# A hand-ordered attention and two-expert kernel on one core: a new order for all of its tasks, written out as a table

## Chip, core and metric

The kernel runs on one core of a Trainium2 chip. Five engines work at once: TensorE (PE in the profile, with PEld for its weight loads), VectorE (DVE), ScalarE (ACT), GpSimd (POOL) and SyncE (SP), which issues all the DMA transfers of this kernel. Each engine takes its own instructions strictly in the order in which the program lists them, and waits on semaphores for the others. The metric is the device time of one execution in microseconds (us); lower is better.

## What is computed

```python
# B, H, S, D = 2, 8, 768, 64: attention masked by equal hash buckets of 6 bits
q_bits = (np.einsum('bhsd,dk->bhsk', q, proj) > 0)          # k_bits alike
mask = q_bucket[:, :, :, None] == k_bucket[:, :, None, :]
scores = np.where(mask, scale * (q @ k.T), -1e9)
attn = exp(scores - max); attn = attn / (sum(attn) + 1e-09); out = attn @ v
# first expert layer, x: 1536 tokens x 512, FF 1536
xn = x / rms * rms_g;  y = (silu(xn @ w_gate) * (xn @ w_val)) @ w_out
# second expert layer, FF 2048
h = y @ w_in;  result = where(h > 0, h, exp(min(h, 0)) - 1) @ w_out2
```

All inputs but the expert matrices are fp32; the expert matrices arrive as 64-bit floats. To keep precision, a matrix product is done in three passes over a high part ("hi", rounded to the matmul's fp32r) and a rest ("lo" = value minus hi): hi*hi, lo*hi, hi*lo.

## The kernel before

**Attention.** The 16 heads are worked as 8 pairs. For a pair, `load_x` loads q and k, transposed to 128 rows (`qk`, `kk`, `qq`: 64 rows of each of two copies). `prep` makes the operands: bits of the hash (`ps_b`, `bitt`), one-hot rows of the mask (`ps_c`, "hot" rows), and the hi and lo parts of k (`operand_k`, tile `tk`) and q (`operand_q`, tile `tq`). A tile `tq` has hi in rows 64 to 127, lo in rows 0 to 63, a second copy of hi ("dup", brought by a small DMA) and the hot rows, so that scores, mask and both precisions come out of four matmuls per 128 queries (`ps_s`, `score`). Then VectorE takes the row maximum (L477, tile `nm`), ScalarE the exponential with its row sum (L487, `p`, `sums`), TensorE transposes p (`ps_p`, `turn`), ScalarE and VectorE (L523, L527; for some tiles ScalarE and GpSimd, L532 to L539) split it into hi and lo (`pt`), TensorE multiplies by v (`ps_v`, `weigh`), and L576 and L580 join the parts. There are 12 score tiles per pair, 96 in all. `post` adds 1e-9 to the 12 row sums of the pair (L598), inverts them (L603), spreads them (`rw`, `ps_x`), and scales the result into `xT` (L629); squares are summed for the norm (`sq`, `ps_z`). `norm` runs after pair 4 for the first batch, on GpSimd, and after pair 8 for the second, on VectorE.

**Experts.** Matrices come in groups of two or three blocks of 128 hidden units (`weights`). Each half matrix is one DMA into `wraw` (L790); ScalarE (L804) and four VectorE instructions (L807, L813, L820, L827) turn the 64-bit words into fp32 (`wf`), ScalarE casts hi (L849, `whi`), GpSimd subtracts for lo (L853, `wlo`). This set of four VectorE instructions is called a conversion below. Then follow `ps_h` (L902), the activation, `ps_y` (L987), and for the second layer `ps_h` and `ps_o` (L1042).

**What sets the order.** Every piece of work is a task (`plan.add`: engine, estimated microseconds, function, keys read and written, priority). `Plan.order` simulates the engines at build time and picks, each time, the task that can start first, with ties broken by priority; the table `OFF` shifts the priorities. `GATE0` names the pair whose first score must be issued before the first group's matrices may load. Buffers are pools of fixed size: 22 `slot` tiles (operands, `p`, `wraw`, `whi`, `wlo`), 14 `h3` tiles.

Of the kernel before, what the change touches and what calls it, by code (L numbers as in the profile page):

```python
# [20 lines left out]
GATE0 = 4  # L21
# [12 lines left out]
class Plan:
# [40 lines left out]
    def order(self):  # L75
        n = len(self.tasks)
        users = [[] for _ in range(n)]
        left = [0] * n
        for i, t in enumerate(self.tasks):
            left[i] = len(t[3])  # L80
            for d in t[3]:
                users[d].append(i)
        free = {tag: [0.0] * c for tag, c in self.caps.items()}
        pending = {b: len(ts) for b, ts in self.touch.items()}
        last = {b: 0.0 for b in self.touch}
        held = set()
        clock = {}
        table = None
        busy = {}
        ready = {}  # L90
        at = [0.0] * n
        end = [0.0] * n

        def put(i):
            eng = self.tasks[i][0]
            clock.setdefault(eng, 0.0)
            ready.setdefault(eng, []).append(i)

        for i in range(n):
            if not left[i]:  # L100
                put(i)
        out = []
        while len(out) < n:
            best = None
            for eng, lst in ready.items():
                now = clock[eng]
                fits = []
                for i in lst:
                    _, us, fn, deps, bufs, prio, lat, tab = self.tasks[i]
                    t = max(now, at[i])  # L110
                    need = {}
                    for b in bufs:
                        if b not in held:
                            need[b[0]] = need.get(b[0], 0) + 1
                    ok = True
                    for tag, c in need.items():
                        fr = free[tag]
                        if len(fr) < c:
                            ok = False
                            break  # L120
                        t = max(t, max(fr[:c]))
                    if ok:
                        fits.append(((t, prio), i))
                if fits:
                    (t, prio), i = min(fits)
                    key = (t, prio, i, eng)
                    if best is None or key < best:
                        best = key
            assert best is not None, "no task can start"
            t, _, i, eng = best  # L130
            _, us, fn, deps, bufs, prio, lat, tab = self.tasks[i]
            ready[eng].remove(i)
            for b in bufs:
                if b not in held:
                    held.add(b)
                    free[b[0]].pop(0)
            if eng == "PE":
                k = int(t / self.WINDOW)
                full = us
                if k < self.COLD or (k > self.COLD and busy.get(k - 1, 0.0) < self.ACTIVE * self.WINDOW):  # L140
                    us = min(2 * us, max(us, us + 0.5 * ((k + 1) * self.WINDOW - t)))
                rate = self.duty[i] * full / us if us else 0.0
                a = t
                while a < t + us:
                    k = int(a / self.WINDOW)
# [1081 lines left out]
```

## Time and profile before

| | |
|---|---|
| runs | 853.52, 851.31, 851.55 us; median 851.55 |
| the profiled execution | 854.81 us by its own time; its span, first to last instruction, 853.0 us |
| busy share of the span | PE 96%, PEld 84%, DVE 73%, ACT 50%, POOL 38% |
| mean granted TensorE clock | 0.988 of full speed |

A busy share is a mean over two very different stages: attention (roughly the first 306 us, to the last `ps_z`) and the experts (the rest). A PE that is busy is not a PE at its peak, since matmuls overlap in the pipeline and a slower clock also counts as busy.

### The profile page before, as it was taken

To read this page: it belongs to the slowest core of one execution; us is meant where nothing else is said; L and a number is where in the kernel's file an instruction comes from. 1 tells how busy PE (TensorE), PEld (TensorE's weight loads), DVE (VectorE), ACT (ScalarE), POOL (GpSimd) and SP (SyncE) were. 2 spreads that over 40 slices of the span, in tenths; PEclk is the share of its full clock that TensorE was granted. 3 is DMA by queue.
4 is the path that set the end of the run, shared out by engine and by line. 5 is a ranking of instruction groups with operands and counts; after the bars stand their busy time and mean duration, and the time that the engine had idled before them with its cause. 6 is when DMAs were issued, how large, how long until landed. Compare 5 with 4: busy or idle time off the path is not lost.

```text
span 853.0 us, 11879 instructions
## 1 busy us (share of the span) xinstructions
PE 822.4 (96%) x4498; PEld 718.0 (84%) x4498; DVE 621.2 (73%) x941; ACT 428.3 (50%) x787; POOL 321.0 (38%) x247
## 2 busy tenths in 40 slices
PE   6989999999889889999999999999999999999998
PEld 5878899888779879989889898888888888888886
DVE  4788899999999997343283665678957778676754
ACT  3868898988688654332231322335544332332321
POOL 6979936578989921121011221210201111111100
PEclk8989999999999989999999999999999999999999
DMA  6334424543102201110210321113222121101003
GB/s 209 102 137 148 149 85 130 168 139 106 54 1 75 75 1 38 62 39 37 74 50 1 114 85 62 42 70 111 75 75 57 58 72 50 50 25 59 16 10 138
DMA packets 28474, 64.99 MB, mean 76 GB/s; under 512 B 2817, under 2 KB 3585, under 8 KB 28417
## 3 DMA queue, kind: packets, MB, share of 16 engines
q1 hardware_dynamic: 28416, 64.24, 23.2%
q8 instruction: 35, 0.57, 0.3%
q14 instruction: 23, 0.18, 0.1%
HBM read 57.94 MB, written 3.15 MB: 72 GB/s over the span
## 4 chain that ended last, share of the span: by engine, by line
PE 65%; DVE 8%; POOL 1%; issue 1%; ACT 1%; DVEq 0%; ACTq 0%
PE ps_h L902 37%; PE ps_o L1042 15%; PE ps_y L987 12%; DVE nm L477 2%; DVE pt L527 1%; DVE wf L820 1%; DVE wf L807 1%; DVE wf L827 1%; PE ps_v L562 1%; ACT pt L523 0%; DVE xT L629 0%; DVE ot L580 0%; PE ps_p L515 0%; POOL xT L724 0%; PE ps_z L667 0%
## 5 line engine op out<-in xcount | busy, mean ns | idle before, releaser
L853 POOL TENSOR_TENSOR wlo<-wf,whi 128x768 fp32r<-128x768 f32 (+1 forms) x54 | 92.3, 1718 | 432.0 <-ACT whi L849 366.7
L902 PE MATMUL ps_h<-xn,whi 128*128 128x512 f32 (+2 forms) x768 | 191.3, 338 | 1.5 <-DVE ot L580 1.5
L902 PEld LDWEIGHTS ps_h<-xn,whi 128*128 128x128 f32 x768 | 134.7, 190 | 14.2 <-DVE ot L580 2.0
L902 PE MATMUL ps_h<-xn,wlo 128*128 128x256 f32 (+2 forms) x384 | 129.3, 337 | 0.0
L1042 PE MATMUL ps_o<-whi,h 128*128 128x512 f32 (+1 forms) x388 | 118.5, 387 | 0.0
L902 PE MATMUL ps_h<-y,whi 128*128 128x512 f32 x384 | 118.2, 389 | 0.0
L927 ACT ACTIVATE sg<-ps_h 128x512 f32<-128x512 f32 (+1 forms) x87 | 50.7, 582 | 117.1 <-PE ps_h L902 115.1
L948 ACT CAST h<-hf 128x512 fp32r<-128x512 f32 (+1 forms) x87 | 51.6, 605 | 113.7 <-DVE hf L933 62.2
L562 PE MATMUL ps_v<-pt,vv 128*128 128x256 f32 x576 | 94.3, 296 | 7.9 <-DVE pt L527 5.2
L477 DVE TENSOR_REDUCE nm<-ps_s 128x1 f32<-128x768 f32 x96 | 90.8, 949 | 11.3 <-PE ps_s L470 10.9
L487 ACT ACTIVATE p<-ps_s,nm 128x768 f32<-128x768 f32 x96 | 87.4, 911 | 21.0 <-DVE nm L477 19.8
L470 PE MATMUL ps_s<-tk,tq 128*128 128x384 f32 x384 | 91.3, 362 | 5.3 <-POOL tq L374 2.2
L562 PEld LDWEIGHTS ps_v<-pt,vv 128*128 128x128 f32 x576 | 79.2, 190 | 15.4 <-DVE pt L527 8.7
L987 PE MATMUL ps_y<-h,whi 128*128 128x512 f32 (+1 forms) x312 | 90.9, 373 | 0.0
L952 DVE TENSOR_TENSOR h<-hf,h 128x512 fp32r<-128x512 f32 (+1 forms) x87 | 67.5, 790 | 27.1 <-ACT h L948 26.5
L515 PE MATMUL ps_p<-ident,p 128*128 128x128 f32 x576 | 82.1, 277 | 4.9 <-ACT p L487 1.5
L1042 PEld LDWEIGHTS ps_o<-whi,h 128*128 128x128 f32 x388 | 72.5, 188 | 15.1 <-DVE oa L1054 0.2
L902 PEld LDWEIGHTS ps_h<-y,whi 128*128 128x128 f32 x384 | 72.1, 188 | 15.1
L527 DVE TENSOR_TENSOR pt<-ps_p,pt 128x512 fp32r<-128x512 f32 x120 | 79.2, 682 | 7.3 <-ACT pt L523 6.4
L849 ACT CAST whi<-wf 128x768 fp32r<-128x768 f32 (+1 forms) x54 | 39.1, 733 | 84.3 <-DVE wf L827 71.9
L902 PEld LDWEIGHTS ps_h<-xn,wlo 128*128 128x128 f32 x384 | 73.1, 190 | 5.7
L515 PEld LDWEIGHTS ps_p<-ident,p 128*128 128x128 f32 x576 | 66.6, 142 | 12.4 <-ACT p L487 2.3
(91 smaller groups left out, 1401.8 us busy)
## 6 DMA issues: line engine op xcount, KB each, us to landing
wraw<-in_moe_w_out_dram SPq DMA_DIRECT2D x12, 768.0 KB, 4.6
qk<-in_heads_dram SPq DMA_DIRECT2D x16, 384.0 KB, 3.5
kk<-in_heads_dram SPq DMA_DIRECT2D x16, 384.0 KB, 5.3
qq<-in_heads_dram SPq DMA_DIRECT2D x16, 384.0 KB, 5.7
wraw<-in_moe_w_in_dram SPq DMA_DIRECT2D x8, 768.0 KB, 4.6
wraw<-in_moe_w_out_dram SPq DMA_DIRECT2D x10, 512.0 KB, 3.4
vn<-in_v_dram SPq DMA_DIRECT2D x8, 384.0 KB, 3.6
wraw<-in_moe_w_gate_dram SPq DMA_DIRECT2D x4, 768.0 KB, 4.5
```

Source lines behind the costliest of these rows:

```text
L470: nc.tensor.matmul(st[B_][:, hf, 0:HS], lhsT=tq[:, x, c * 128:(c + 1) * 128], rhs=tk[:, x, hf * HS:(hf + 1) * HS], start=(x == 0), stop=(x ...
L477: nc.vector.tensor_reduce(out=st["nm", u, cc], in_=st[B_][:, :, 0:HS], axis=AX.XY, op=ALU.max, negate=True,)
L487: nc.scalar.activation(out=halves(st["p", u][:, cc]), in_=st.pop(B_)[:, :, 0:HS], func=AF.Exp, bias=st["nm", u, cc], scale=1.0, accum_out= ...
L515: nc.tensor.transpose(out=st[B_][:, o:o + 128], in_=p[:, cc, (2 * n + kt) * 128:(2 * n + kt + 1) * 128], identity=ident,)
L527: nc.vector.tensor_tensor(out=pt[:, 1], in0=st.pop(B_), in1=f(pt[:, 0]), op=ALU.subtract)
L562: nc.tensor.matmul(st[B_][:, 0:256], lhsT=st["vv", j][:, a, 2 * n + kt, :], rhs=pt[:, x, kt * 256:(kt + 1) * 256], start=(n == seq[0] and ...
L853: nc.gpsimd.tensor_tensor(out=l, in0=s["w"], in1=f(h), op=ALU.subtract)
L902: nc.tensor.matmul(ps[:, o:o + ln], lhsT=w[wp][:, kk, ft * 128:(ft + 1) * 128], rhs=t[xp][:, s:s + ln], start=(kk == 0 and n == 0), stop=( ...
L948: nc.scalar.copy(out=st["h", g, blk, ft][:, 0, 0:bw], in_=s["hf"])
L952: nc.vector.tensor_tensor(out=h[:, 1, 0:bw], in0=s["hf"], in1=f(h[:, 0, 0:bw]), op=ALU.subtract)
L987: nc.tensor.matmul(s["ps"][:, 0:bw], lhsT=wo[wp][:, ft, m * 128:(m + 1) * 128], rhs=h[:, xp, 0:bw], start=(ft == 0 and i == 0), stop=(ft = ...
L1042: nc.tensor.matmul(s["ps"], lhsT=h[:, xp, t * 128:(t + 1) * 128], rhs=wo[wp][:, ft, ds], start=(ft == 0 and i == 0), stop=(ft == n - 1 and ...
```

## The change

- The order of all 2,732 tasks is written out as a list, `ORDER`; `Plan.order` is gone, and `run` follows the list. `OFF` has other numbers, and is no longer used to order.
- `GATE0` goes from 4 to 2 (counted from 0): the first group's loads may be issued from the third pair on, before from the fifth.
- The hi part of q, before one GpSimd instruction on 128 rows with a scale per row from the tile `share` (L354, scale 1 above, 1/8 below), becomes two GpSimd instructions on 64 rows: a copy (`upper`) and a multiplication by a constant (`lower`). The dup DMA now waits for `lower` alone, lo for `upper` alone.
- The addition of 1e-9 to the 12 sums goes from VectorE to GpSimd.
- Estimates in `plan.add` change; they no longer have an effect once the order is a list.

```diff
-GATE0 = 4
+GATE0 = 2
...
-QENG = [("Pool", "SP", "Pool", "Pool")] * 16
...
+QENG = ["Pool"] * 16
...
+ORDER = [
+    9, 0, 6, 5, 1, 7, 56, 50, 53, 2, 8, 48, 51, 57, 59, 49, 28, 10, 12, 13, 14, 15, 16, 17, 54, 55, 11, 60, 61, 68,
...
-    def order(self):
...
     def run(self):
-        for i in self.order():
+        assert sorted(ORDER) == list(range(len(self.tasks)))
+        for i in ORDER:
             self.tasks[i][2]()
...
-        def hi():
-            cast(engs[0], operand(j, a, 0)[:, 0, cs], st["x", j, a, 2][:, cs], share[:, 1:2])
...
+        def upper():
+            out, in_ = operand(j, a, 0)[up, 0, cs], st["x", j, a, 2][up, cs]
+            nc.gpsimd.tensor_copy(out=out, in_=in_)
+
+        def lower():
+            out, in_ = operand(j, a, 0)[dn, 0, cs], st["x", j, a, 2][dn, cs]
+            if how == "mixed":
+                nc.scalar.activation(out=out, in_=in_, func=AF.Copy, scale=QSCALE)
             else:
...
+                nc.gpsimd.tensor_scalar(out=out, in0=in_, scalar1=QSCALE, scalar2=None, op0=ALU.mult)
...
+        his, los, dups = ([okey(j, a, 0, (p, h)) for h in cols] for p in ("hi", "lo", "dup"))
...
+            plan.add("Pool", 0.12 + n * 0.00092, upper, [X_], los, prio)
...
+                plan.add("Pool", 0.12 + n * 0.00092, lower, [X_], his, prio)
+        dma(dup, 64 * n * 4, his, dups, prio)
+        plan.add("Pool", pool(n), lo, [X_], los, prio)
...
         def plus():
             st[R_] = sml.tile([128, 2, NC], F32, tag="r", name="r")
-            nc.vector.tensor_scalar(
+            nc.gpsimd.tensor_scalar(
                 out=st[R_], in0=st["sum", j], scalar1=1e-9, scalar2=None, op0=ALU.add,
             )
...
-        plan.add("DVE", 0.18, plus, sums, [R_], prio)
+        plan.add("Pool", 0.12, plus, sums, [R_], prio)
```

The line numbers of the changed kernel are 47 or 48 higher in most places (L477 becomes L524, L527 L574, L807 to L827 L854 to L874, L629 L676, L647 L694).

**GpSimd, first pair.** Its first instructions that work on q and k, before:

```order
L334 TENSOR_TENSOR tk<-kk,tk 64x384
L354 TENSOR_SCALAR tq<-qq,share 128x384 x2
L374 TENSOR_TENSOR tq<-qq,tq 64x384 x2
L334 TENSOR_TENSOR tk<-kk,tk 64x384
L293 CAST vv<-vn 128x6x64 x2
L299 TENSOR_TENSOR vv<-vn,vv 128x6x64 x2
```

and now (L405 is `upper`, L412 `lower`, L420 q's lo, L382 k's lo):

```order
L405 CAST tq<-qq 64x384 x2
L420 TENSOR_TENSOR tq<-qq,tq 64x384
L412 TENSOR_SCALAR tq<-qq 64x384 x2
L420 TENSOR_TENSOR tq<-qq,tq 64x384
L382 TENSOR_TENSOR tk<-kk,tk 64x384 x3
L405 CAST tq<-qq 64x384 x2
L412 TENSOR_SCALAR tq<-qq 64x384
L341 CAST vv<-vn 128x6x64 x2
```

The first head's q now comes before all of k; before, k's first half stood ahead of it. On SP the first transfer is now `qq` (before the sixth), and the two `qk`, before first and second, are second and fourth.

**VectorE, end of attention.** Before, from the last row maximum (`nm`) on, up to the second square (L651), which the last `ps_z` reads; L807 to L827 are conversions:

```order
L477 TENSOR_REDUCE nm<-ps_s 128x1
L827 SCALAR_TENSOR_TENSOR wf<-wraw,wf 128x768
L807 TENSOR_SCALAR wf<-wf 128x768
L580 TENSOR_TENSOR ot<-ps_v,ot 64x256
L813 TENSOR_SCALAR wf<-wf 128x768
L598 TENSOR_SCALAR r<-sums 128x12
L820 SCALAR_TENSOR_TENSOR wf<-wraw,wf 128x768
L603 RECIPROCAL r<-r 128x12
...
L813 TENSOR_SCALAR wf<-wf 128x768
L647 TENSOR_TENSOR sq<-xT 128x768
L820 SCALAR_TENSOR_TENSOR wf<-wraw,wf 128x768
L651 TENSOR_TENSOR sq<-sq 128x768
```

and now, from the last two row maxima on:

```order
L524 TENSOR_REDUCE nm<-ps_s 128x1 x2
L574 TENSOR_TENSOR pt<-ps_p,pt 128x512
L627 TENSOR_TENSOR ot<-ps_v,ot 64x256
L574 TENSOR_TENSOR pt<-ps_p,pt 128x512
L874 SCALAR_TENSOR_TENSOR wf<-wraw,wf 128x768
L574 TENSOR_TENSOR pt<-ps_p,pt 128x512 x3
...
L650 RECIPROCAL r<-r 128x12
L980 TENSOR_TENSOR hf<-ps_h,sg 128x384 x2
...
L676 TENSOR_TENSOR xT<-ot,ps_x 128x384 x2
L694 TENSOR_TENSOR sq<-xT 128x768
L698 TENSOR_TENSOR sq<-sq 128x768
```

Between the last maximum and the second square there were 13 instructions of conversions; now there is one. The first instruction of a conversion, before behind 52 of the 96 row maxima, is now behind 32, and the first two conversions are complete behind 51.

**SP, third and fourth pair.** The changed order, with tile numbers (`tq_963` is the q operand of the second head of the fourth pair):

```order
L416 DMA tq_1053<-tq_1053 64x768
L837 DMA wraw_1141<-in_moe_w_gate_dram 128x2x384
L837 DMA wraw_1145<-in_moe_w_gate_dram 128x2x384
L837 DMA wraw_1208<-in_moe_w_out_dram 128x3x256
L837 DMA wraw_1210<-in_moe_w_out_dram 128x3x256
L416 DMA tq_963<-tq_963 64x768
L322 DMA qk_1284<-in_heads_dram 128x768
```

Before, all dup transfers up to that of the fifth pair stood ahead of the first load of a matrix; now four loads stand ahead of this one.

## Rows read from the trace of the kernel before

**Rows 1.** Busy time of each engine in stretches of the span: us, count; granted clock.

```profile
core 0: us, PE busy (x) PEld busy (x) DVE busy (x) ACT busy (x) POOL busy (x), PEclk, DMA share, GB/s
0.00:25.00 25.00, 18.35 (x84) 15.16 (x85) 12.28 (x21) 10.96 (x21) 16.43 (x23) 0.86 0.64 212
25.00:50.00 25.00, 21.51 (x146) 19.51 (x145) 20.69 (x29) 19.22 (x40) 23.79 (x22) 0.98 0.47 161
50.00:75.00 25.00, 23.71 (x142) 21.31 (x142) 18.71 (x29) 19.20 (x39) 20.33 (x18) 0.89 0.39 129
300.00:306.00 6.00, 3.23 (x6) 2.00 (x7) 6.00 (x9) 1.88 (x4) 3.38 (x2) 0.61 0.00 0
306.00:849.00 543.00, 543.00 (x2677) 468.55 (x2676) 350.39 (x544) 188.67 (x313) 76.27 (x47) 1.00 0.17 57
```

**Rows 2.** The same view, attention cut at 147 us and at the last row maximum.

```profile
16.40:147.00 130.60, 124.33 (x821) 113.17 (x821) 108.68 (x161) 108.76 (x221) 104.17 (x92) 0.95 0.38 126
147.00:276.20 129.20, 121.22 (x826) 106.82 (x825) 125.00 (x189) 109.73 (x219) 105.78 (x79) 1.00 0.30 92
276.20:302.80 26.60, 19.36 (x122) 18.39 (x121) 26.25 (x28) 13.92 (x23) 25.30 (x17) 0.97 0.19 60
```

**Rows 3.** Timeline, first pair: start, length, engine, line, tiles, idle time before.

```profile
8.32 1.12 ACT L327 ACTIVATE tk<-kk,share 128x384 fp32r<-128x384 f32 x2 [6.32 <-DMA kk<-in_heads_dram]
11.51 0.48 ACT L423 ACTIVATE tk<-ps_c 64x384 fp32r<-64x384 f32 x1
10.19 2.48 POOL L354 TENSOR_SCALAR tq<-qq,share 128x384 fp32r<-128x384 f32 x2
12.63 1.96 POOL L374 TENSOR_TENSOR tq<-qq,tq 64x384 fp32r<-64x384 f32 x2
13.66 0.79 PE L470 MATMUL ps_s<-tk,tq 128*128 128x384 f32 x3 [2.19 <-POOL tq L374]
15.70 1.97 PE L470 MATMUL ps_s<-tk,tq 128*128 128x384 f32 x5 [1.25 <-POOL tk L334]
```

**Rows 4.** DMA issues of the first 16 us: KB each, median us to landing.

```profile
qk<-in_heads_dram SPq DMA_DIRECT2D x4, 384.0 KB, 3.5
```

**Rows 5.** Timeline around the first L598, VectorE; then a wait of TensorE, 25 to 50 us.

```profile
45.46 3.58 DVE L598 TENSOR_SCALAR r<-sums 128x12 f32<-128x12 f32 x1
48.95 0.68 DVE L527 TENSOR_TENSOR pt<-ps_p,pt 128x512 fp32r<-128x512 f32 x1
PE ps_v L562 <- DVE pt L527: 1.9, 1, 1.9
```

**Rows 6.** Line L598: shortest, median, longest ns; first and last start.

```profile
L598 DVE TENSOR_SCALAR r<-sums x8: 165/536/3580, 45.5 to 280.8; 128x12 f32<-128x12 f32 x8
```

**Rows 7.** Groups by line: busy us, mean ns of one, idle before.

```profile
L354 POOL TENSOR_SCALAR tq<-qq,share 128x768 fp32r<-128x768 f32 (+1 forms) x18 | 36.1, 2007 | 1.2 <-POOL tk L334 0.6
L611 POOL COPY rw<-r 128x768 f32<-128x768 f32 x8 | 6.8, 850 | 5.9 <-DVE r L603 3.2 <-DVE xT L629 2.6
L694 POOL TENSOR_SCALAR z<-z 128x384 f32<-128x384 f32 x2 | 1.6, 804 | 0.2
L293 POOL CAST vv<-vn 128x384 fp32r<-128x384 f32 x16 | 7.8, 507 | 0.1
```

**Rows 8.** Stretches again, VectorE instructions on tile wf (the conversions) alone.

```profile
0.00:147.00 147.00, 0.28 (x1) 0.95 0.42 137
147.00:277.10 130.10, 21.63 (x19) 1.00 0.30 91
277.10:303.50 26.40, 15.79 (x13) 0.96 0.19 60
```

**Rows 9.** Timeline of the tail, VectorE; then the waits of TensorE there.

```profile
295.07 2.59 DVE L647 TENSOR_TENSOR sq<-xT 128x768 f32<-128x768 f32 x1
297.58 2.57 DVE L820 SCALAR_TENSOR_TENSOR wf<-wraw,wf 128x768 int32<-128x768 int32 x1
300.08 2.55 DVE L651 TENSOR_TENSOR sq<-sq 128x768 f32<-128x768 f32 x1
302.77 2.90 PE L667 MATMUL ps_z<-sq,ones 128*128 128x384 f32 x4 [4.35 <-DVE sq L651]
```

**Rows 10.** Waits of SP's own queue: total us, times, longest.

```profile
SPq L790 <- PE ps_s L470: 9.4, 1, 9.4
SPq L367 <- POOL tq L354: 113.6, 18, 17.6
```

More of the change, by code (lines that the diff above doesn't have):

```diff
@@ L34 @@
+ORDER = [
[140 rows of a table added]
+]
 class Plan:
@@ L73, in add @@
         return i
-    def order(self):
[L76 to L145, printed above, removed]
-                    z = min(t + us, (k + 1) * self.WINDOW)
-                    if z <= a:
-                        k, z = k + 1, min(t + us, (k + 2) * self.WINDOW)
-                    busy[k] = busy.get(k, 0.0) + (z - a) * rate
-                    a = z
-            if tab is not None and tab != table:
-                table = tab
-                us += self.TABLE
-            clock[eng] = t + us
-            end[i] = t + us + lat
-            for b in bufs:
-                pending[b] -= 1
-                last[b] = max(last[b], end[i] + self.HOP)
-                if not pending[b]:
-                    free[b[0]].append(last[b])
-            for u in users[i]:
-                left[u] -= 1
-                at[u] = max(at[u], end[i] + self.HOPS.get((eng, self.tasks[u][0]), self.HOP))
-                if not left[u]:
-                    put(u)
-            out.append((t, i))
-        self.span = max(clock.values())
-        self.placed = out
-        return [i for _, i in out]
@@ L348, in operand_q, with both @@
         n = HS * len(cols)
[L350 to L362 removed]
+        def both():
+            nc.scalar.activation(
+                out=operand(j, a, 0)[:, 0, cs], in_=st["x", j, a, 2][:, cs], func=AF.Copy, scale=share[:, 1:2]
+            )
@@ L365, in dup @@
             t = operand(j, a, 0)
[L366 to L369 removed]
+            nc.sync.dma_start(out=f(t[dn, 1, cs]), in_=f(t[dn, 0, cs]))
         def lo():
             t = operand(j, a, 0)[up, 0, cs]
[L373 to L374 removed]
@@ L376, in operand_q @@
-        plan.add(engs[0], us(engs[0]), hi, [X_, "share"], [okey(j, a, 0, (p, h)) for p in ("hi", "lo") for h in cols], prio)
-        duped = [okey(j, a, 0, ("dup", h)) for h in cols]
-        if engs[1] == "SP":
-            dma(dup, 64 * n * 4, [okey(j, a, 0, ("hi", h)) for h in cols], duped, prio)
-        else:
-            plan.add(engs[1], us(engs[1]), dup, [X_, "share"], duped, prio)
-        plan.add(
-            engs[2], pool(n) if engs[2] == "Pool" else dve(n), lo, [X_],
-            [okey(j, a, 0, ("lo", h)) for h in cols], prio,
-        )
+            nc.gpsimd.tensor_tensor(out=t, in0=st["x", j, a, 2][up, cs], in1=f(t), op=ALU.subtract)
@@ new lines, in operand_q @@
+        his, los, dups = ([okey(j, a, 0, (p, h)) for h in cols] for p in ("hi", "lo", "dup"))
+        if how == "ACT":
+            plan.add("ACT", act(n) + 0.15, both, [X_, "share"], his + los, prio)
+        else:
+            plan.add("Pool", 0.12 + n * 0.00092, upper, [X_], los, prio)
+            if how == "mixed":
+                plan.add("ACT", act(n) + 0.05, lower, [X_], his, prio)
+            else:
+                plan.add("Pool", 0.12 + n * 0.00092, lower, [X_], his, prio)
+        dma(dup, 64 * n * 4, his, dups, prio)
@@ L770, in wpart, with weights @@
         return t[:, part * (KD // 2):(part + 1) * (KD // 2), :]
-    def weights(g, m, part, prio, gate):
+    def weights(g, m, part, prio, gate, late=None):
         li, f0, n, _, _ = groups[g]
```

44 lines of the change are left out of this document (15 added, 29 removed), and 139 rows, old and new, of the table ORDER.

## The prediction

> **What bounds the kernel now.** I cut the span into stretches first [rows 1]. From 306 to 849 us TensorE is busy 543.00 of 543 us at full clock: the experts are bound by matmuls, which the change neither removes nor adds. Nothing can be won there, and something can be lost only if a matrix comes late. All that can move lies before the last `ps_z`, which starts at 302.77 us [rows 9].
>
> In that stage I asked for each part of it which engine is full [rows 2]. From 16.4 to 147 us TensorE is busy 124.3 of 130.6 us, VectorE 108.7, GpSimd 104.2: TensorE leads, VectorE has 22 us to spare. From 147 us to the last row maximum at 276.2 VectorE is busy 125.0 of 129.2 us, TensorE 121.2: now VectorE leads. In the tail to 302.8 us VectorE is busy 26.25 of 26.6 us, while TensorE has 19.4 us of work. Why VectorE is so full late is in the rows of the conversions: a quarter of a microsecond before 147 us, then 19 instructions (21.6 us) to the last maximum and 13 (15.8 us) in the tail [rows 8]. They stand in front of the two squares that the last `ps_z` needs, and one of them, 2.57 us long, stands between the squares; TensorE waits 4.35 us for the second square [rows 9] and then runs at a clock of 0.61 in the mean, part of it at the lower level, 1.2 GHz [rows 1].
>
> The other losses are early. TensorE has 18.35 us of work in the first 25 us [rows 1]: the first score begins at 13.66 us, when GpSimd has made q's lo, and stands again until 15.70 for k's lo [rows 3]. And at 45.46 us a VectorE addition on 12 columns takes 3.58 us; behind it L527 comes late and TensorE waits 1.9 us [rows 5]. In the 25 us from 50 on the mean clock is 0.89, although TensorE is busy 23.7 of them [rows 1].
>
> **The addition (L598).** Eight of these, of one shape, take 165 to 3580 ns [rows 6]. The same 12 columns need 165 ns at best; the rest is a wait inside the instruction, and the longest falls into the 25 us in which GpSimd is busy for 23.8 [rows 1]. The Trainium skill (SBUF — State Buffer, "SBUF: two separate sides") says that VectorE and GpSimd take a shared port pair as an exclusive lock, for a whole instruction, and the second fully blocks. The 3580 ns agree with that. The same skill (Perfetto Trace Analysis, "Optimizing Scalar/DVE Operations") warns that moving work between these two engines might not help, which would bring the first rival's time, and so speaks against this edit. By the rows: with the addition on GpSimd the wait of 3.58 us cannot happen on VectorE. That is worth the 1.9 us of TensorE's wait, and the clock lost after it: 25 us at 0.89 is 2.75 us of full speed. Term B: **4.6 us**, bounds 0 and 4.7. The cost is eight short GpSimd instructions that wait for the last exponential of a pair; behind them stand the next q and `pt` parts. No row shows this instruction on GpSimd; the nearest is L694, a `TENSOR_SCALAR` of 384 columns, mean 804 ns [rows 7]. From nothing to 8 x 0.8 = 6.4 us of GpSimd time; I take it as covered in the stretch where it first stands, since from 16.4 to 276.2 us GpSimd has 50 us idle [rows 2]; without that cover it costs those 6.4 us.
>
> **The start.** Before, one GpSimd chain stands between k's arrival (ScalarE starts on it at 8.32 us) and the first score: k's lo, 2.48 us of q's hi, 1.96 of q's lo, k's lo again [rows 3]. Now `qq` is the first transfer. The first transfers, `qk` before, land 3.5 us after issue [rows 4], so q is there at about 4.3 us, and GpSimd does two copies (0.51 each [rows 7]), two multiplications of the same length, and 1.96 us of lo, 4.0 us, before k arrives. What is left is two halves of k's lo after ScalarE's 1.12 us, so the score is ready on that side at about 8.3 + 0.8 (256 KB more ahead of k, at the rate below) + 1.1 + 1.0 = 11.2 us. The other side is the hot rows: they ended at 11.99 us [rows 3], and hang on both `qk`, which come one transfer of 384 KB later than before. The first 25 us move 212 GB/s at a DMA share of 0.64 [rows 1], so 331 GB/s while something moves, and 384 KB take 1.2 us. So 13.2 us in place of 15.70, with half a microsecond for the clock behind the wait term A: **3 us**, bounds 0 (if `qk` is late by 3 us) and 5.
>
> **q's two steps, elsewhere.** L354 takes 36.1 us in 18 instructions; one of 768 columns is about 2.2 us, since four of the 18 have 384 columns and take 1.24 [rows 3, 7]. No row shows the new pair at 768 columns. Below: L611, a copy with 768 columns, takes 0.85 us [rows 7], so two steps 1.7. Above: the multiplication is still a `TENSOR_SCALAR`, and if it costs by columns as L354 does, 2.2 each, 4.4 for two. I take 1.7, since L694, also a `TENSOR_SCALAR`, but with constants, has a mean of 0.8 us for 384 columns with waits in it [rows 7], and copies are nearer. That relieves GpSimd by 0.5 x 14 + 0.2 x 4 = 8 us. I count it at nothing: GpSimd leads in no part of rows 2. If it were 4.4, it would be the second rival.
>
> **The new order, 147 us to the last maximum.** By the changed order, two whole conversions (8 instructions) are done behind 51 maxima, so ahead of about 147 us, and in all 23 conversion instructions stand ahead of the last maximum, where there were 19. So 15 are left where 19 stood: 4 x 1.14 us (21.63 / 19 [rows 8]) = 4.6 us less. Three L598 go with some 1 us. Five L527 at 0.68 [rows 5] and a few smaller ones move behind the last maximum, 5 us. VectorE's 125 us become 114. If it stays as full as it is (97%), the stretch takes 118 us and not 129. But GpSimd, 106 us less a few, and TensorE then stand close behind, and three engines that are nearly equal wait for each other more. Term C: **9 us**, bounds 0 (if these waits eat it) and 13.
>
> **Ahead of 147 us** VectorE gets the two conversions, 9.1 us, and loses four L598 (most of it the 3.58); it has 22 us idle there [rows 2]. TensorE leads in this stretch, and each conversion put in front of a maximum can delay it by its length. Cost E: **2 us**, bounds 0 and 6.
>
> **The tail.** Of the 13 conversion instructions one is left, 14 us less for VectorE; about 5 us of L527 and smaller ones come in. VectorE's 26 us become 16 or less, TensorE's matmuls from the last score to `ps_z` grow by about 2.7 us, since fewer are done before. So TensorE leads: its idle 7.2 us [rows 2] shrink to perhaps 2 (the squares still meet GpSimd's subtractions, and may stay 2.5 us long). Term D: 5 less 2.7, and 1.4 us for the lower clock after the wait (half of about 2.9 us of `ps_z` [rows 9]), together **3.9 us**, bounds -3 and 7.
>
> **Sum.** 3 + 4.6 + 9 - 2 + 3.9 = 18.5 us. Against the profiled execution's own 854.81 us (its span is 853.0) that is 836.3; that execution lies 3.3 us above the median of 851.55, so I predict **833** for the median. The experts' 543 us stay.
>
> **Rivals.**
> 1. *The lock takes it back.* The conversions still run beside GpSimd, which now takes the port for two steps of q where it took it once, and for the additions; their waits only move to other instructions. Then C is nothing and B halves: 3 + 2.3 - 2 + 1 = 4 us, 847. For it: L820 takes 2.57 us [rows 9] where a conversion's instruction has a mean of 1.14 [rows 8]; against it: the long addition itself is gone, and 12 of the 13 instructions that had such waits in the tail.
> 2. *GpSimd becomes the bound (slower).* If a step of q costs what L354 cost on 128 rows, 2.2 us, GpSimd gets 14 x 2.2 + 4 x 1.24 = 36 us more. It is 92% busy from 25 to 50 us and 95% in the tail [rows 1, 2]. Its 245 us up to the last `ps_z` become about 280 of 303; with some 60% of the steps in stretches where it is near full, 22 us appear on the path, against the 18.5 won: 855. It decides from about 3.9 us for the two steps together. For it: same kind of instruction, same columns; against it: L611 and L293 [rows 7].
> 3. *A dup behind expert loads.* Four loads now stand ahead of a dup on SP; an expert load has waited 9.4 us for scores [rows 10], and dups wait for q's hi anyway, 113.6 us in 18 waits, so SP is not ahead of time. If that dup is 10 us late, TensorE stands and the clock falls: 10 + 2.7 us off the gain at one place, about 846. Against it: five scores lie between.
> 4. *TensorE nearly full.* All VectorE idle time ahead of 147 us is used well and C reaches its upper end, D too: 3 + 5 + 13 + 7 + a bit = 30 us, 821 or less.
>
> **Chances.** The forecast's mechanism with its size, 822 to 846: 0.70. Rival 4, under 822: 0.10. Rival 1, at 847: 0.04. Rival 3, at 846 or a little over: 0.03. Within 0.3% of before (849 to 854; 0.3% is about what a measurement of this kernel can tell from no change), when A to D all come at their low ends: 0.05. Slower: rival 2 0.06, another cause 0.02. The span of 822 to 846 leaves out 3 in 10; I widen it to 820 to 848, which takes in rivals 1 and 3 and part of rival 4, and leaves out some 2 in 10. Faster is 0.70 + 0.10 + 0.07 = 0.87.
>
> **What the profile will show.** A: the first score before 13 us, with no wait of about 2 us for GpSimd. B: no VectorE instruction of 12 columns over 0.3 us, and clock 1.00 from 50 to 75 us. q: the copy and the multiplication at 768 columns under 1 us each. C: VectorE's share from 75 to 147 us above 92%, the last maximum at about 255 to 262 us. D: the second square's wait under 2 us. Experts: TensorE 100% busy from the last `ps_z` on, 543 us. The prediction is wrong if a q step takes 2 us, if TensorE's waits for `pt` parts grow by as much as VectorE is relieved, or if TensorE waits in the experts for a matrix.

## The result, and the profile after

| | before | changed |
|---|---|---|
| median of 4 runs, us | 852.48 (851.31 to 853.52) | 840.04 (839.08 to 841.96) |
| the profiled execution's own time, us | 854.81 | 840.58 |
| span of its trace, us | 853.0 | 838.8 |
| last `ps_z` begins at, us | 302.77 [rows 9] | 288.79 |

The ratio is 0.9857, 95% interval [0.9832, 0.9882]: 12.4 us faster by the medians, 14.2 by the profiled executions. The forecast was 18.5 us and 833. From the last `ps_z` to the end it is 550.0 us in place of 550.2: as predicted, all of the gain lies in the attention. Two executions far above the rest of their run, 1011.53 us in e1 and 4487.47 us in e3, are left out of the times below.

The stretches below answer to [rows 2]. The second cut is at 141.0 us, where TensorE has as much work left to the last `ps_z` as it had at 147 us before: 115.32 + 24.10 = 139.4 us here, 121.22 + 0.97 x 19.36 = 140.0 there. The last two rows answer to [rows 1], and to a place of which the experiments speak.

```profile
14.70:141.00 126.30, 121.52 (x809) 109.92 (x808) 109.48 (x167) 109.73 (x222) 115.24 (x100) 0.97 0.48 151
141.00:264.70 123.70, 115.32 (x798) 102.91 (x796) 116.60 (x175) 102.93 (x212) 108.40 (x94) 1.00 0.20 60
264.70:288.80 24.10, 24.10 (x163) 24.00 (x163) 15.13 (x23) 14.24 (x27) 16.45 (x16) 1.00 0.28 99
...
50.00:75.00 25.00, 24.72 (x179) 23.10 (x178) 21.36 (x33) 22.77 (x50) 24.11 (x21) 1.00 0.38 127
200.00:225.00 25.00, 21.54 (x143) 18.35 (x142) 22.94 (x38) 17.83 (x36) 23.25 (x19) 1.00 0.18 48
```

Read TensorE's idle time in each stretch, length less busy, beside that of [rows 2]:

| | before | changed | won, us |
|---|---|---|---|
| first row maximum begins | 16.43 | 14.69 | 1.7 |
| idle to 147 / 141 us | 6.3 | 4.8 | 1.5 |
| idle from there to the last maximum | 8.0 | 8.4 | -0.4 |
| idle in the tail | 7.2 | 0 | 7.2 |
| busy from the first maximum to the last `ps_z` | 264.9 | 260.9 | 4.0 |

The sum is 14.0 us. TensorE's busy time falls because less of it runs below full clock (0.89 before from 50 to 75 us [rows 1], now 1.00). So the gain has two ends, the start with the addition's stretch and the tail; the middle, from which the forecast took half of its sum, gives nothing.

A part of the first row belongs to this one execution of the kernel before, which lies 2.3 us above its median. Two runs with the same old start, e4 and e9 below, begin their first maximum at 15.48 and 15.44 us; two with the new start, e10 and e12, at 14.90 and 15.24. In the means of three traces each the start is worth 0.8 us.

The groups of GpSimd's instructions, by shape (busy us, mean ns | idle before), then TensorE's longest waits from 141 to 265 us (total, times, longest), then the same of before, from 147 to 276.2 us:

```profile
L412 POOL TENSOR_SCALAR tq<-qq 64x768 fp32r<-64x768 f32 x14 | 29.9, 2133 | 1.2
L420 POOL TENSOR_TENSOR tq<-qq,tq 64x768 fp32r<-64x768 f32 x14 | 26.5, 1891 | 0.6
L405 POOL CAST tq<-qq 64x768 fp32r<-64x768 f32 x14 | 11.9, 848 | 0.4
...
L645 POOL TENSOR_SCALAR r<-sums 128x12 f32<-128x12 f32 x8 | 3.1, 385 | 5.0 <-ACT p L534 4.5
```

```profile
PE ps_s L517 <- ACT p L534: 3.0, 4, 1.4
PE ps_p L562 <- DVE pt L574: 2.0, 5, 0.7
PE ps_c L461 <- DVE pt L574: 1.0, 1, 1.0
```

```profile
PE ps_v L562 <- DVE pt L527: 3.3, 7, 1.1
PE ps_p L515 <- ACT p L487: 1.5, 2, 0.9
PE ps_x L620 <- DVE tk L425: 0.9, 1, 0.9
PE ps_s L470 <- ACT p L487: 0.9, 2, 0.5
```

q's two steps take 0.85 + 2.13 = 2.98 us for 768 columns, not 1.7. And of TensorE's idle time in the middle, by the whole of these two lists, the waits for VectorE are 4.9 us now and were 4.7 before; those for ScalarE are 3.0 and were 2.7. VectorE has less to do there, and TensorE waits for it as long as before.

### The profile page after: what moved, and what is told of

Read it like the earlier page. It is cut to its first block, busy times and chain, and to the rows that moved or that the text cites. A ratio compares the mean times of both kernels' runs of the same rounds, so it can differ in the third digit from the quotient of the medians.

```text
span 838.8 us, 11843 instructions
## 1 busy us (share of the span) xinstructions
PE 816.9 (97%) x4498; PEld 714.1 (85%) x4498; DVE 602.1 (72%) x933; ACT 416.8 (50%) x785; POOL 328.1 (39%) x273
## 4 chain that ended last, share of the span: by engine, by line
PE 77%; DVE 11%; ACT 7%; issue 2%; POOL 1%; DMA 1%; SPq 0%; ACTq 0%; DVEq 0%; POOLq 0%
PE ps_h L949 36%; PE ps_o L1089 15%; PE ps_y L1034 10%; PE ps_v L609 5%; PE ps_s L517 5%; PE ps_p L562 4%; DVE pt L574 2%; DVE nm L524 2%; ACT p L534 2%; ACT pt L570 2%; PE ps_b L442 1%; DVE wf L867 1%; DMA kk<-in_heads_dram 1%; DVE wf L874 1%; DVE ya L1046 1%
## 5 line engine op out<-in xcount | busy, mean ns | idle before, releaser
L900 POOL TENSOR_TENSOR wlo<-wf,whi 128x768 fp32r<-128x768 f32 (+1 forms) x54 | 88.4, 1650 | 448.3 <-ACT whi L896 387.4
L949 PE MATMUL ps_h<-xn,wlo 128*128 128x512 f32 (+2 forms) x384 | 128.9, 336 | 0.0
L524 DVE TENSOR_REDUCE nm<-ps_s 128x1 f32<-128x768 f32 x96 | 90.8, 947 | 7.4 <-PE ps_s L517 6.5
L999 DVE TENSOR_TENSOR h<-hf,h 128x512 fp32r<-128x512 f32 (+1 forms) x87 | 64.5, 756 | 41.5 <-ACT h L995 41.3
L574 DVE TENSOR_TENSOR pt<-ps_p,pt 128x512 fp32r<-128x512 f32 x120 | 80.0, 682 | 12.9 <-ACT pt L570 12.0
L562 PE MATMUL ps_p<-ident,p 128*128 128x128 f32 x576 | 84.6, 278 | 2.9 <-DVE pt L574 2.2
L517 PEld LDWEIGHTS ps_s<-tk,tq 128*128 128x128 f32 x384 | 64.3, 191 | 14.9 <-ACT p L534 10.8
```

Of the source, the lines that this page charges most:

```text
L517: nc.tensor.matmul(st[B_][:, hf, 0:HS], lhsT=tq[:, x, c * 128:(c + 1) * 128], rhs=tk[:, x, hf * HS:(hf + 1) * HS], start=(x == 0), stop=(x ...
L524: nc.vector.tensor_reduce(out=st["nm", u, cc], in_=st[B_][:, :, 0:HS], axis=AX.XY, op=ALU.max, negate=True,)
L562: nc.tensor.transpose(out=st[B_][:, o:o + 128], in_=p[:, cc, (2 * n + kt) * 128:(2 * n + kt + 1) * 128], identity=ident,)
L574: nc.vector.tensor_tensor(out=pt[:, 1], in0=st.pop(B_), in1=f(pt[:, 0]), op=ALU.subtract)
L900: nc.gpsimd.tensor_tensor(out=l, in0=s["w"], in1=f(h), op=ALU.subtract)
L949: nc.tensor.matmul(ps[:, o:o + ln], lhsT=w[wp][:, kk, ft * 128:(ft + 1) * 128], rhs=t[xp][:, s:s + ln], start=(kk == 0 and n == 0), stop=( ...
```

## The experiments

**The addition, both ways.** `nc.gpsimd` and `nc.vector` exchanged in `plus`, in either kernel, the order kept.

```
# e4: before                     # e1, e12: changed
-  nc.vector.tensor_scalar(      -  nc.gpsimd.tensor_scalar(
+  nc.gpsimd.tensor_scalar(      +  nc.vector.tensor_scalar(
       out=st[R_], in0=st["sum", j], scalar1=1e-9, ...
```

> The kernel before with nothing changed but the engine of the eight additions, in the same order. Theory of the held port: the 3.58 us at 45 us are gone, the granted clock from 50 to 75 us rises from 0.89 to 1.00, and the time falls by 3 to 5 us, to 848 to 849.5. Rival, the additions' wait costs nothing or only moves to another VectorE instruction with operands in SBUF: 851 to 853.

847.99 us, ratio 0.9957 [0.9943, 0.9972]; the clock from 50 to 75 us is 1.00. The addition alone is worth 3.5 us in the old order. Run e9, which leaves this part of the kernel before as it was, shows what it is made of: it starts level with e4, its addition takes 3.59 us, TensorE waits 1.9 us behind it as in [rows 5], and at the 17th of the 96 row maxima it is 3.0 us behind e4 (59.18 against 56.18 us). Its clock:

```profile
50.00:75.00 25.00, 23.47 (x150) 20.68 (x149) 19.44 (x31) 20.69 (x43) 21.35 (x19) 0.96 0.39 128
```

So the same wait cost 1.0 us of clock here (25 us at 0.96), and not the 2.75 of the execution profiled before.

> The changed kernel with the eight additions on 12 columns back on VectorE, at the same places of the order. Theory of the held port: a VectorE instruction with all operands in SBUF can not start its work while GpSimd runs one instruction behind the other, and gets it in GpSimd's next gap. In the changed kernel GpSimd is busy 24.1 of 25 us from 50 to 75 us, so at least one of the eight additions should take over 1 us, the next subtraction that reads ps_p comes late, and the time is 2 to 5 us above 840.0. Rival, the order alone made the gain and the addition's wait was chance: all eight under 0.5 us, and 839 to 841.

844.11 us, ratio 0.9916 [0.99, 0.9933]: 4.1 us above the changed kernel, as the first theory said. For the place the kernel was run again.

> The changed kernel with the eight additions on 12 columns on VectorE once more, since the profile of the first run of it had TensorE at a clock of 0.75 throughout and shows no place. That run was 4.4 us slower than the changed kernel, while the one without any addition, where VectorE's reciprocal of the same 12 columns waits for the same exponentials, was 1 us faster. If the port makes the difference: an addition of over 1 us, or an instruction from SBUF to SBUF behind it that meets a subtraction on GpSimd and takes 1 us more than in the changed kernel, with a wait of TensorE for pt parts or a lower clock in the same 25 us, and 843 to 845.5. If the additions only add their own 1.3 us and the order of waits: no such instruction, the loss spread over the pairs, 0.3 to 0.8 us each.

845.14 us (2 runs), 5.1 above the changed kernel. VectorE's timeline (start, length):

```profile
73.38 1.22 DVE L645 TENSOR_SCALAR r<-sums 128x12 f32<-128x12 f32 x1 [1.30 <-ACT p L534]
...
95.31 1.70 DVE L854 TENSOR_SCALAR wf<-wf 128x768 f32<-128x768 f32 x1 [0.18 <-ACT wf L851]
...
109.23 1.94 DVE L854 TENSOR_SCALAR wf<-wf 128x768 f32<-128x768 f32 x1
```

One addition takes over 1 us; the other waits in additions are 0.39 and 0.59 us, and three below 0.2. In front of the long one VectorE also stands 1.30 us for the pair's last exponential, a wait that it does not have there in the changed kernel. The row maxima show where e12 loses, against the changed kernel: 1.6 us at this addition, where it falls from 0.5 us ahead to 1.1 behind; 0.8 more by 150 us; 0.6 at the addition of 173.79 us; and 2.6 from 205 to 231 us, where the clock falls to 0.93 from 200 to 225 us (1.00 in the changed kernel).

The 0.8 us come with the two L854 behind the addition, 0.70 and 0.54 us long in the changed kernel and 1.70 and 1.94 here: they come 0.8 and 1.8 us later and meet a GpSimd subtraction. They can't be the main price, since e6 below has the same two at 1.70 and 1.95 and is as fast as the changed kernel. So of the loss less than half is made at the additions, and there the wait inside the instruction and the wait for the exponential in front of it come together; no run parts the two. The largest piece is made at a place 30 us later than the last long addition, to which we come back. The loss is measured; that the port makes all of it is not shown.

**The addition left out.** `inv` reads the sums itself.

```
-  nc.vector.reciprocal(out=st[R_], in_=st[R_])
+  nc.vector.reciprocal(out=st[R_], in_=st["sum", j])
```

> The changed kernel without the addition of 1e-9 (each of the 12 sums is at least 1, since its row's maximum is subtracted, so that in fp32 the addition changes nothing), the reciprocal reads the sums. In the changed kernel GpSimd does the eight additions in 3.1 us and stands 4.5 us for exponentials ahead of three of them, with q and pt parts behind it. If that costs: 837 to 839. If it is covered: 839.5 to 841. A new collision on the port: up to 843.

839.03 us (838.92 to 839.12), 0.9848 [0.983, 0.9866]. At most 1 us: on GpSimd the addition is as good as free.

**The price of q's steps.** Once the old single instruction (the tile `share` that it reads is set up earlier), once a cheaper form of the second step.

```
# e2:  128 rows, in place of both steps
+  nc.gpsimd.tensor_scalar(out=out, in0=in_, scalar1=share[:, 1:2], scalar2=None, op0=ALU.mult)
# e3:
-  ... scalar1=QSCALE, scalar2=None, op0=ALU.mult)
+  ... scalar1=QSCALE, scalar2=0.0, op0=ALU.mult, op1=ALU.add)
```

> The changed kernel with q's hi again as one GpSimd instruction on 128 rows, in the place of the first of its two steps. The two steps cost 0.82 and 2.13 us at 768 columns in the changed kernel, the one step cost 2.2 us before, so GpSimd should lose 10 to 12 us of 328. If GpSimd bounds no stretch (the prediction counted the steps at nothing): 838 to 841. If its added time stands on the path in the stretches where it is near full: 832 to 837. If the early upper half is what let the first score start sooner: the first row maximum up to 1 us later, and 841 to 842.

> The changed kernel with the lower step of q's hi as a multiplication and an addition of 0 in one instruction, as in the Newton step, which takes 0.51 us on 128 rows and 384 columns and writes plain fp32. If the form with one operation is what costs 2.13 us at 768 columns: 0.85 to 1.1 us for this one, GpSimd some 15 us less busy, and the time 835 to 840. If it is the written type (rounded fp32r) or the rows 64 to 127: again 2.0 to 2.3 us, and 839 to 841.

Both make GpSimd cheaper and the kernel slower: e2 843.77 us, 0.9911 [0.9894, 0.9928]; e3 843.47 us, 0.9907 [0.9891, 0.9924]. In e3 the lower step takes 0.89 us, so the form with one operation is what costs 2.13, and GpSimd is busy 306.0 us, not 328.1; still 3.4 us are lost, which neither theory had. From 150 to 209 us e3's row maxima come 0.3 us later than the changed kernel's (between 95 and 145 us 0.5 to 1.9 later, which it gets back), and by 231 us 3.2 later. In between, at one place, on VectorE and GpSimd, first the changed kernel:

```profile
212.40 0.63 DVE L854 TENSOR_SCALAR wf<-wf 128x768 f32<-128x768 f32 x1
...
214.15 0.55 DVE L854 TENSOR_SCALAR wf<-wf 128x768 f32<-128x768 f32 x1
...
211.80 2.13 POOL L412 TENSOR_SCALAR tq<-qq 64x768 fp32r<-64x768 f32 x1
214.01 2.36 POOL L420 TENSOR_TENSOR tq<-qq,tq 64x768 fp32r<-64x768 f32 x1
```

and e3, with TensorE's wait behind it (last row):

```profile
213.03 1.46 DVE L854 TENSOR_SCALAR wf<-wf 128x768 f32<-128x768 f32 x1
...
215.60 0.99 DVE L854 TENSOR_SCALAR wf<-wf 128x768 f32<-128x768 f32 x1
...
212.25 1.83 POOL L420 TENSOR_TENSOR tq<-qq,tq 64x768 fp32r<-64x768 f32 x1
214.23 1.94 POOL L382 TENSOR_TENSOR tk<-kk,tk 64x768 fp32r<-64x768 f32 x1 [0.16 <-ACT tk L375]
...
217.35 0.62 PE L461 MATMUL ps_c<-bitt,wsel 128*128 128x384 f32 x2 [1.52 <-DVE pt L574]
```

GpSimd is earlier, so the same two conversion steps now start inside its subtractions and do their own work when these end (212.25 + 1.83 = 214.08; the step ends at 214.49). TensorE waits 1.52 us, 1.0 in the changed kernel, and the clock in these 25 us is 0.93. e2 loses 3.9 us at the same place: there the second of the two steps takes 2.16 us inside a subtraction, and TensorE waits 2.6. The test is to give back the dear form at this place only, for the two tiles of pair 7.

```
# e6, in front of the branch with one operation
+  elif j < 7:
+      nc.gpsimd.tensor_scalar(... scalar2=0.0, op0=ALU.mult, op1=ALU.add)
```

> The cheap form of q's lower step (0.89 us) for pairs 0 to 6, and the dear form (2.13 us) for the two tiles of pair 7 alone, which stand at 208 to 214 us in the changed kernel. With the cheap form everywhere a conversion's instruction at 213 us met GpSimd's subtraction of q and took 1.46 us in place of 0.55, a second one at 215.6 took 0.99; TensorE waited 1.5 us there, its clock fell to 0.93, and 3.5 us were lost. Theory of the collision: the loss is made at this place; with the dear form there the two conversion instructions run beside it again in 0.55 to 0.65 us, the clock from 200 to 225 us is 1.00, and the time 839 to 841, although GpSimd is 15 us less busy. Rival, the loss comes from GpSimd being early in general (other orders of waits): 843 to 844 as with the cheap form everywhere.

839.92 us, 0.9856 [0.9841, 0.9871], clock 1.00 from 200 to 225 us, and the two steps take 0.63 and 0.54 us. The collision theory holds; that GpSimd being early in general costs time does not. And what GpSimd saves in all (328.1 to 308.2 us busy) wins nothing: the forecast's cover was right, its price was not.

**The port by itself.**

> The changed kernel with a stage of its own ahead of all other work, for its trace alone: on GpSimd, one form after the other, 8 casts of 64 rows and 768 columns to rounded fp32, 4 multiplications in the form with one operation, 8 in the form with two, 4 subtractions of two tensors, 8 copies of 128 rows in fp32, 4 multiplications of 128 rows by a pointer; beside each on VectorE ten pairs of a maximum with a constant on 768 columns and an addition on 12, all from SBUF to SBUF. If only subtractions hold VectorE up: its instructions take 0.55 and 0.16 us beside all other forms, and wait for the end of the instruction beside subtractions. If every GpSimd instruction holds the port: waits beside all forms. If a waiting VectorE instruction must find a gap between two GpSimd instructions: one of them waits for the whole row of subtractions (some 7 us), otherwise for one of them at a time (1.8 us). Without VectorE beside them the forms should cost 0.82, 2.13, 0.89, 1.8, 0.82 and 2.2 us.

The kernel's time (912.77 us, one execution) says nothing here; its first 76 us are read. GpSimd's rows, then VectorE's first ones beside the multiplications with one operation, beside the subtractions, and after these:

```profile
1.52 9.32 POOL L1235 CAST pr<-pa 64x768 fp32r<-64x768 f32 x8
...
14.82 9.76 POOL L1237 TENSOR_SCALAR pr<-pa 64x768 fp32r<-64x768 f32 x4
...
26.93 9.82 POOL L1239 TENSOR_SCALAR pr<-pa 64x768 fp32r<-64x768 f32 x8
...
38.99 7.29 POOL L1241 TENSOR_TENSOR pr<-pa 64x768 fp32r<-64x768 f32 x4
...
17.41 0.67 DVE L1253 TENSOR_SCALAR po<-pd 128x12 f32<-128x12 f32 x1
18.11 0.56 DVE L1252 TENSOR_SCALAR po<-pd 128x768 f32<-128x768 f32 x1
...
41.11 1.31 DVE L1253 TENSOR_SCALAR po<-pd 128x12 f32<-128x12 f32 x1
42.46 0.56 DVE L1252 TENSOR_SCALAR po<-pd 128x768 f32<-128x768 f32 x1
...
46.94 0.17 DVE L1253 TENSOR_SCALAR po<-pd 128x12 f32<-128x12 f32 x1
```

Every form holds VectorE up, not subtractions alone: 12 columns take 0.17 us when GpSimd is still, 0.67 beside casts and multiplications, 1.31 beside subtractions. The two engines take turns, one instruction each: none waits for a whole row of them. GpSimd pays as well: the first cast takes 0.82 us and those with VectorE between them 1.24, the first subtraction 1.46 and the others 1.87. And four multiplications with one operation take as long as eight with two, and VectorE gets the port eight times beside them too: the dear form behaves like two instructions. The Trainium skill (SBUF — State Buffer, "SBUF: two separate sides") has the holder keep the pair for its whole instruction while the other fully blocks. The subtractions agree with that (at 41.11 us an addition has 1.28 us of one ahead of it and waits 1.14); the form with one operation does not, it lets VectorE in halfway. The first theory of this run falls, the second holds; to the question of the third, VectorE waits for one instruction at a time.

**The start.** Pair 0 alone: q's lower step first, in the cheap form (as in e6, with `j == 0`); hot rows ahead of the second tk.

```
-  9, 0, 6, 5, 1, 7, 56, 50, 53, 2, 8, 48, 51, 57, 59, ... 11, 60, 61, 68, ... 42, 43, ... 46, 39, 41, 30, 72, 74, 75, 38, 37, 44, 76,
+  9, 0, 6, 5, 1, 7, 51, 50, 53, 2, 8, 48, 57, 56, 59, ... 11, 68, ... 42, 37, 43, ... 46, 60, 61, 39, 38, 41, 30, 72, 74, 75, 44, 76,
```

> The changed kernel with another order in the first microseconds, for pair 0 alone: q's lower step first (so that its duplicate is sent sooner), as a multiplication and an addition of 0 in one instruction; on VectorE the first hot rows of tq ahead of ScalarE's; on ScalarE the hot rows of tk ahead of the second tk's hi. In the changed kernel TensorE stands from 11.97 to 14.07 us in the first score, for these hot rows. If these are what it waits for: third to eighth matmul of the scores about 2 us sooner, the first row maximum at 12.5 to 13 us in place of 14.69, and 837.5 to 838.5 if what is won stays won. Rival, the first 25 us are bound by the transfers: maximum at 14 us or later, 839.5 to 841. Where the engines' shift against each other makes a new collision on the port, as in the run with two operations, up to 843.

837.77 us (837.24 to 838.5), 0.9828 [0.9814, 0.9843]. TensorE's first scores, changed kernel and e5:

```profile
14.07 1.55 PE L517 MATMUL ps_s<-tk,tq 128*128 128x384 f32 x6 [2.10 <-DVE tq L472]
```

```profile
12.37 1.28 PE L519 MATMUL ps_s<-tk,tq 128*128 128x384 f32 x6 [0.33 <-DMA tq<-tq]
```

The first maximum begins at 12.99 us, and the clock of the first 25 us is 1.00, not 0.86. At 186 us e5 is 3.6 us ahead; from 200 to 225 us it waits as the changed kernel does (1.0 and 1.36 us), but here the clock falls to 0.93, and 2.3 us are left.

**That place at 210 us.** On top of e5, two exponentials and two conversion steps moved.

```
# e11, in the list of tasks
  ... 1088, +1171, ... 1480, +1168, ... -1493 ... -1485 ... -1168, -1171, 1281, 1283, +1493, +1485, ...
```

> The run with the other start (837.8), and at 207 to 217 us two exponentials of one tile ahead of ScalarE's work for the next pair, and two conversion steps (maximum with a constant) on VectorE behind the hot rows of pair 7. There TensorE waited 1.0 us for a subtraction of pt and 1.36 us for an exponential, and the clock fell to 0.93 in the 25 us from 200 on. If these two orders make the waits: both gone, clock 1.00, 834.5 to 836.5. If the exponentials were put late for lack of a buffer, or the next wait comes at once: 837 to 839.

842.65 us, and the runs lie 6 us apart (839.42 to 845.68; 0.9902 [0.9867, 0.9937]): it is slower than e5, and above both ranges of the expectation. The fastest of the four has the trace, and shows this on ScalarE:

```profile
207.94 0.90 ACT L510 ACTIVATE p<-ps_s,nm 128x768 f32<-128x768 f32 x1 [2.98 <-DVE wf L850]
```

The exponential, put early, waits 2.98 us for a conversion's last step: that step reads `wraw`, which shares its pool of slots with `p`. So it had stood late for lack of a buffer. Why the other three runs lose up to 6 us more, no trace shows.

**What the conversions cost.** In the changed kernel all four VectorE steps are left out; in the kernel before only those of the three conversions in the tail.

```
# e7: c2, c3, c4, c5 replaced by an empty step
# e9, at the head of c2, c3, c4, c5:
+  if (g, m, part) in ((0, 2, 1), (1, 0, 0), (1, 0, 1)):
+      return
```

> The changed kernel without VectorE's four steps of every weight conversion (it leaves out that part of the computation; ScalarE's step, scaled down to keep the numbers finite, and all that reads the result stay). In the attention VectorE loses 24.3 us of about 253, most of it from 145 to 265 us. If VectorE bounds that stretch, as the prediction read it in the kernel before: the last ps_z 8 to 15 us sooner, 826 to 832. If TensorE's own work and its waits for exponentials do: 836 to 839. The experts stay 100% TensorE either way.

832.05 us, 0.9763 [0.9746, 0.9779], close to the first theory's bound: 24.3 us less for VectorE in the attention go with 8 us. But not all 8 are won there by the conversions. The profiled execution is already 2.2 us ahead at 50 us, before any conversion would have begun, and wins 2.0 behind the last `ps_z` (548.0 us to the end, not 550.0). From the 49th to the last row maximum it takes 123.8 us where the changed kernel takes 127.9: 4.1 us. The last `ps_z` comes 7.5 us sooner, a little less than the 8 to 15 of the first theory. TensorE's waits of that kernel from 135 to 257 us:

```profile
PE ps_s L517 <- ACT p L534: 3.5, 6, 1.4
PE ps_p L562 <- DVE pt L574: 0.5, 2, 0.3
```

All its waits for VectorE there are 1.8 us, in place of 4.9; those for ScalarE's exponentials are 3.5, in place of 3.0.

> The kernel before without VectorE's four steps of the three conversions that stand behind or around the last maximum (12 instructions, some 15 us; it leaves out that part of the computation). This does to the tail what the change does to it, and nothing else. If VectorE holds the last ps_z up, as the prediction read it (term D, 3.9 us, bounds to 7): the wait of 4.4 us for the second square is gone, the lower clock behind it too, and the time is 846 to 849 beside 852. If the tail is bound by TensorE or by GpSimd's 25 of 26.6 us: 851 to 853.

843.73 us, 0.9902 [0.9883, 0.992]: 8.3 us, twice what the forecast gave the tail. From the last maximum to the last `ps_z` it takes 19.1 us, not 26.5. The wait of 4.4 us is gone, the squares take 0.96 and 1.66 us in place of 2.59 and 2.55 [rows 9]. Leaving work out is worth more than moving it, so this is an upper price; the changed kernel, which moves it, has 7.2 us of idle time less there.

## Why the prediction was right, and where its sum was not

Direction, place and range were right (840 in 820 to 848); the sum was 4.3 us too large on the executions' own times. That it came so near is in part luck: the start and the middle gave 8 us less than forecast, the tail and the stretch ahead of 147 us some 4 more. By its steps:

- **Start, 3 us forecast, 1.7 measured, 0.8 in the means.** GpSimd's chain did shrink. The next in line was not late q or k but the hot rows: ScalarE had a second tk ahead of them, and VectorE's stood behind ScalarE's, until 14.07 us. e5 gets 2.3 us more, so the bound of 5 was fair.
- **Addition, 4.6 forecast, 3.5 (e4) and 4.1 (e1) measured.** Right in size, and in the old order right in mechanism: e4 and e9 differ by the wait of 1.9 us and its clock. The clock's 2.75 us were those of one execution; e9 lost 1.0. That 3580 ns "agree" with a lock held for a whole instruction was misread: GpSimd's longest instruction beside it takes 1.26 us, and the wait spans four. In the changed order (e12) less than half of the loss is made at the additions.
- **q's two steps, 1.7 us taken, 2.98 measured.** The step that failed is "copies are nearer": the multiplication costs 2.13, near L354's 2.2. "Under 1 us each" was wrong, and a step of 2 us was one of the prediction's own signs of being wrong. It did no harm: rival 2 had the right price for this step, but the two stayed under its threshold of 3.9 us, and e6 shows that the cover was there.
- **Middle, 9 forecast (term C), nothing measured.** This is where the sum failed. 2.7 of the 9 were matmuls that the tail takes over (term D pays for them), so 6.3 us of TensorE's idle time were booked. VectorE did lose work (125.0 to 116.6 us busy in the stretch), and I let the stretch shrink with it, "if it stays as full as it is". But TensorE was idle for 8.0 us there [rows 2], and only 4.7 of these were waits for VectorE. VectorE's share fell to 94%, TensorE's idle time stayed at 8.4 us, 4.9 of it waits for VectorE: these hang on where single instructions stand, not on VectorE's sum. Even with no conversion left on VectorE (e7) the stretch is only 4.1 us shorter than in the changed kernel; 6.3 were booked for moving a few of them away.
- **Tail, 3.9 forecast (term D), 7.2 of idle time measured.** In idle time the forecast was 5: I expected 2 us of wait to stay and squares of up to 2.5 us. GpSimd, 25.3 of 26.6 us busy before, is at 16.45 of 24.1, so the squares meet nothing and take 0.96 each; TensorE is full.
- **Ahead of 147 us, a loss of 2 us forecast.** It does not show: this stretch won 4.3 us (1.5 idle, 2.8 busy), a little more than the addition alone.

C and D together booked 11.3 us of the 15.2 idle us that [rows 2] show after 147 us, and 6.8 came. Of the rivals, the lock (1) was not what took C: a conversion's instruction has a mean of 1.01 us (24 take 24.28) and not 1.14 [rows 8]. Rival 3 did not show: from 16 to 290 us no wait of TensorE ends with a DMA. The shares named as tests: clock 1.00 from 50 to 75 us held, no wait at the second square held, no VectorE instruction of 12 columns over 0.3 us held (the longest is 0.22); VectorE's share from 75 to 147 us is 91% (65.79 of 72), just short of the 92; the first score began at 11.46 us, but stood from its third matmul on; the last maximum came at 264.72 us and not by 262.

Three readings of the rows were off, with little weight: GpSimd is 95% busy from 25 to 50 us [rows 1], not 92; of the 13 conversion instructions of the tail the last begins at 302.6 us, behind the second square, so 12 stood in front of it; and the first of the 19 ahead of the last maximum begins at 146.7 us, so the order took three, not four, out of the stretch behind 147 us.

## What to carry to other kernels

When work leaves an engine that seems to lead a stretch, first take the idle time of the engine that sets the end, in that stretch, and split it by what ended each wait: here 8.0 us, of which 4.7 were waits for VectorE, where I booked 6.3. Even these need not go, since a wait hangs on where one instruction stands in the order. Where two engines share a port, the price of an instruction includes where it starts: making GpSimd 22 us cheaper cost 3.4 us, because two VectorE steps of 0.6 us slid into subtractions, and two instructions kept dear at that place gave it back. So in an order written out for one timing, change one thing, and compare the two traces by milestones (here the 96 row maxima) to find the first place where they part. And a single profiled execution has a start and a clock of its own: read them in a second trace of the same order before a term is built on them.

## What the runs showed of the hardware

- A VectorE instruction from SBUF to SBUF that starts inside a GpSimd instruction on two tensors takes longer, in most cases, by what is left of that one less 0.13 us: 1.66 for 1.79 left, 1.40 for 1.54, 0.82 for 0.95 in the kernel before; beside casts and copies of the changed kernel too (0.29 for 0.42, 0.43 for 0.55). Not always: the step at 214.15 us above begins 0.14 us behind a subtraction and takes its usual 0.55, and the subtraction takes 2.36 us in place of 1.8, so there VectorE had its turn first. Row maxima (0.89 to 0.96 us) and instructions that read PSUM never did, nor the reciprocal on 12 columns (0.21 to 0.23 in both kernels).
- One operation costs GpSimd more than two: 2133 ns against 890 for 64 rows and 768 columns, even more than a subtraction of two tensors (1891). The Trainium skill (GPSIMD Engine Reference, "Engine selection") has two-input elementwise work about twice as slow there and one-input work at about line rate; the cast agrees (848 ns), this multiplication does not.
- Left open: the first addition before, 3.58 us at 45.46 us [rows 5], spans four GpSimd instructions, where in e8 none waits for more than one:

```profile
44.99 1.26 POOL L539 TENSOR_TENSOR pt<-pf,pt 128x512 fp32r<-128x512 f32 x1
46.21 0.60 POOL L536 CAST pt<-pf 128x512 fp32r<-128x512 f32 x1
46.78 1.01 POOL L299 TENSOR_TENSOR vv<-vn,vv 128x384 fp32r<-128x384 f32 x1
47.75 1.25 POOL L539 TENSOR_TENSOR pt<-pf,pt 128x512 fp32r<-128x512 f32 x1
```

It ends, at 49.04, with the last of them (49.00), and e9 shows it again with 3.59 us; why it did not get its turn earlier no run here shows. Also open is the clock from 200 to 225 us: e5 has the changed kernel's waits there and 0.93, the changed kernel 1.00; e10 has the two conversion steps as long as e12 has them (0.85 and 1.00 against 0.85 and 1.01) and 1.00, e12 0.93. e10 loses 0.7 us at this place and e12 2.6.
